# A cast and four copies moved to GpSimd, five steps moved within their lists, and a last product in two halves (attention and gated MLP, one core)

## The chip, the cores and the metric

The kernel runs on one core of one Trainium2 chip. A core has TensorE (PE in the profile; its weight loads are PEld), VectorE (DVE), ScalarE (ACT), GpSimd (POOL) and SyncE (SP), which here issues the transfers between the chip's memory and the core's SBUF. Every engine works through its own list of instructions in order and waits for the others by semaphores. The metric is the time of one execution in microseconds; lower is better.

## The reference

Eight batches, eight heads, 576 positions, head size 64. First attention in which a position sees itself and the 63 before it:

```
scores = matmul(q, k^T) / 8;  keep where 0 <= row - col < 64
attn   = exp(scores - max) / (sum + 1e-9)
x      = matmul(attn, v)          # heads side by side: [8, 576, 512]
```

Then a gated MLP with a product over positions:

```
h   = relu(x @ w_in)              # 1024 wide; u = first half, v = second half
v_n = (v - mean(v)) / sqrt(var(v) + 1e-6)
v_s = w_spatial @ v_n + b_spatial # over the 576 positions
out = (u * v_s) @ w_out           # [8, 576, 512], float32
```

All inputs and the output are float32; products are done in float16 with float32 sums.

## The kernel before

The code describes the work as named steps. The string ORDER is written out by hand: it lists every step once, with its engine and the numbers of the buffers it takes. The steps are issued in this order, so the list of each engine is the subsequence of ORDER with its name; DQ means a transfer on SP's queue. An engine's list is strict: an instruction that waits holds up all that are behind it. The names carry batch, head group (0 or 1, four heads each) and part.

For each batch and group:

- ldq, ldk, ldv load q, k (one transfer each, into one of eight buffers `nat`) and V (five transfers, positions in chunks of 128). The transfers of SP use eight semaphores in turn, so a transfer waits for the one issued eight places before it.
- cq, ck cast q and k to float16 (`cp`, line 301, or 293 on ACT; on POOL in three pieces of 384, line 296), tq, tk transpose them on DVE (line 408). cv casts V into `hv`; sl, su and s4 copy it into `hs`, shifted by half a chunk (lower half of the partitions, upper half, the last 64 positions). In batches 0 and 1 cv, sl and su come in two parts, 0 and 1 (su1_10 is batch 1, group 1, part 0).
- S (PE, line 470) makes the scores, E (ACT, line 477) their exp, M (DVE, line 480) applies the mask as a minimum, Z (PE, line 493) sums over columns, N and n (ACT, lines 519 and 521) give the inverse as exp of minus log, P (PE, line 504) multiplies with V from hv and hs, and X (DVE, line 512) scales into x. The steps with _r do the last 64 positions of both groups.

For each batch then:

- V (PE, line 643) makes the second half of h, Vr the relu (ACT, line 623), Vb and Va mean and variance (DVE, lines 625 and 627), L1 and L2 the inverse root (ACT), A the rescaling (DVE, line 682).
- U (PE, line 698) and Ur (ACT, line 711) make the first half, G (PE, line 728, the last columns 734) the product over positions, Ge (DVE, line 742) multiplies by u.
- O (PE, line 753) is the last product, Oe (ACT, line 606) copies it out of PSUM, st stores it. The last 64 positions of a batch share a step with V of the next batch (V_4: lines 656 and 659); those of batch 7 have none and are O7_4 (line 765): four products of 64 output rows and 512 columns, copied by Oe7_4 and stored by st7_4.

The three weights are loaded and cast between batches 0 and 1 (ldwin, cwin; ldwsp, cwsp, then W and We, which transpose the spatial weights; ldwo, cwo). ldb loads the spatial bias, cb casts it. NWARM = 25 pairs of products D on a scratch tile fill TensorE's waits in batch 0.

PSUM has two pairs of banks (for S) and four single banks, whose numbers 0 to 3 stand behind each PE step in ORDER. A step that takes a bank waits until the last reader of its former content is done: P1_11 takes bank 1, which Ge0_2 empties, and G0_2 takes bank 1, which X1_01 empties.

Of the kernel before, what the change touches and what calls it, by code (L numbers as in the profile page):

```python
# [13 lines left out]
B = 8  # L14
# [13 lines left out]
ldwin101:DQ D8:PE:1 su0_01:DVE sl0_01:POOL n0_10:ACT su0_10:DVE D13:PE:2 ldwin000:DQ:1 n0_01:ACT
tk1_0:DVE:5 s40_0:POOL ldk1_1:DQ:2 N0_11:ACT:4 P0_01:PE:3 ldq1_1:DQ:3 P0_00:PE:1 n0_11:ACT
cv0_11:DVE ldwin001:DQ S1_0:PE:0:1 sl0_11:DVE X0_00:DVE:0 D20:PE:2 cwin110:POOL ldwin010:DQ:4  # L30
E1_00:ACT:1 s40_1:DVE D19:PE:0 ldwin011:DQ su0_11:POOL X0_01:DVE ldwsp3:DQ:5 E1_01:ACT:0 M1_00:DVE
# [17 lines left out]
su1_11:DVE n1_r:ACT Ge0_2:DVE:2 P1_10:PE:2 n1_11:ACT X1_10:DVE:3 ck2_1:POOL:2 P1_11:PE:1 ldk3_0:DQ:2
S2_0:PE:1:0 X1_11:DVE cwo10:ACT ldv2_01:DQ P1_r:PE:2 Ge0_0:DVE:3 V1_2:PE:1 E2_00:ACT:0 X1_r:DVE:1  # L50
Ge0_1:DVE:4 E2_01:ACT:1 V1_1:PE:3 cq2_1:POOL:3 ldv2_02:DQ tk2_1:DVE:0 V1_3:PE:2 Vr1_2:ACT:5
ldv2_03:DQ cwo00:POOL Vr1_1:ACT:6 tq2_1:DVE:1 U1_2:PE:0 ldv2_10:DQ:1 Vr1_3:ACT:7 cwo11:ACT
ldv2_11:DQ V1_0:PE:1 M2_00:DVE Ur1_2:ACT:5 Vb1_2:DVE:5 cwo01:ACT S2_1:PE:1:0 Vr1_0:ACT:4 M2_01:DVE
Z2_00:PE:3 cq3_0:POOL:0 ldv2_04:DQ E2_10:ACT:3 V1_4:PE:2 Vb1_1:DVE:1 ldv2_12:DQ Va1_2:DVE
# [115 lines left out]
class Plan:  # L170
# [27 lines left out]
def kernel(  # L198
# [11 lines left out]
    nc = tc.nc  # L210
# [55 lines left out]
    w_out_sb = [cpool.tile([128, 512], f16, name=f"wout{r}") for r in range(4)]  # L266
# [331 lines left out]
    def out_steps(b, j, m, po, key, rows):  # L598
        half = j % 2
        if half == 0:  # L600
            OB[b] = (buf("ob", f"ob{b}_{j}") if j < 4 else buf("ob4", f"ob{b}_4")), None
        ob, first = OB[b]

        def view():
            return ob.t[rows, half, :] if j < 4 else ob.t[rows, :]
        cpy = add(f"Oe{b}_{j}", ("ACT", 0.49), key, lambda e: nc.scalar.copy(view(), m.t[rows, :]),  # L606
                  deps=[po, first], acq=[] if half else [ob], uses=[m] + ([ob] if half else []))
        OB[b] = ob, cpy
        if j == 4:
            add(f"st{b}_4", ("DQ", 0.45), key, lambda e: nc.sync.dma_start(  # L610
                out[b, 512:576, :], view()), deps=[cpy], uses=[ob], nbytes=0.4, n=64)
# [22 lines left out]
    def gmlp_steps(b, key):  # L634
        VS, ST, VN = [], [], []
        for j in range(4):
            m = buf("bank", f"pv{b}_{j}")
            vs = buf("vs", f"vs{b}_{j}")

            def emit_V(e, j=j, m=m):  # L640
                with nc.named_scope(f"V{b}_{j}"):
                    for r in range(4):
# [32 lines left out]
        for j in range(5):  # L675
# [4 lines left out]
            def emit_A(e, j=j, jn=jn, vn=vn):  # L680
# [8 lines left out]
        for i in range(5):  # L689
            m = buf("bank", f"pu{b}_{i}")  # L690
            ru = buf("ru", f"ru{b}_{i}")
            n = 512 if i < 4 else 256

            def emit_U(e, i=i, m=m):
                with nc.named_scope(f"U{b}_{i}"):
# [4 lines left out]
                    else:  # L700
                        for c in range(4):
                            for r in range(4):
# [10 lines left out]
        G = []
        gd = []
        for i in range(5):
            m = buf("bank", f"pg{b}_{i}")
            g = buf("g", f"g{b}_{i}")
            n = 512 if i < 4 else 256
            ru, rd = RU[i]

            def emit_G(e, i=i, m=m):
                def vk(kk):
                    return (VN[kk].t[:, :], 128) if kk < 4 else (vn4_t[b % NSB][:, :], 65)
                with nc.named_scope(f"G{b}_{i}"):
# [5 lines left out]
                    else:  # L730
                        for c in range(4):
                            for kk in range(5):
# [6 lines left out]
                     deps=AP + WSP, acq=[m], uses=[vn for vn in VN if vn], mode="f")  # L739
            gd.append(pg)  # L740
            G.append((g, add(f"Ge{b}_{i}", ("DVE", 0.07 + 0.00105 * n), key + 0.4 + 0.03 * i,
                             lambda e, m=m, g=g, ru=ru, n=n: nc.vector.tensor_tensor(  # L742
                                 g.t[:, 0:n], m.t[:, 0:n], ru.t[:, 0:n], ALU.mult),
                             deps=[pg, rd], acq=[g], uses=[m, ru])))
        GDONE[b] = gd
        G4[b] = G[4]
        for j in range(4):
            m = buf("bank", f"po{b}_{j}")

            def emit_O(e, j=j, m=m):  # L750
                with nc.named_scope(f"O{b}_{j}"):
                    for r in range(4):
                        nc.tensor.matmul(m.t[:, :], G[r][0].t[:, 128 * j:128 * j + 128],  # L753
                                         w_out_sb[r][:, :], start=(r == 0), stop=(r == 3))
            po = add(f"O{b}_{j}", ("PE", 0.866), key + 0.7 + 0.03 * j, emit_O,
                     deps=[G[r][1] for r in range(4)] + WOUT, acq=[m],
                     uses=[G[r][0] for r in range(4)], mode="f")
            out_steps(b, j, m, po, key + 0.7 + 0.03 * j, slice(0, 128))
        if b == B - 1:
            m = buf("bank", f"po{b}_4")  # L760

            def emit_O4(e, m=m):
                with nc.named_scope(f"O{b}_4"):
                    for r in range(4):
                        nc.tensor.matmul(m.t[0:64, :], G[4][0].t[:, 64 * r:64 * r + 64],
                                         w_out_sb[r][:, :], start=(r == 0), stop=(r == 3))
# [60 lines left out]
```

## Time and profile before

| what | value |
|---|---|
| median of 3 runs | 203.99 us (203.55 to 204.42) |
| the profiled execution | 204.42 us |
| its span, first to last instruction | 202.6 us |
| granted TensorE clock | 0.999 |
| PE busy | 189.1 us, 93% |
| ACT busy | 167.9 us, 83% |
| DVE busy | 162.4 us, 80% |
| POOL busy | 74.0 us, 37% |
| read from memory, written | 32.79 MB, 9.44 MB |

Busy times and shares are sums over the whole span; the slices and the windows of the trace tell in which stage an engine is full. The chain of waits follows the work that ended last back from the end of the span: at each step to what released it, or to the instruction before it on its engine. In the timeline, a row is a group of like instructions that follow each other: start, length, engine, line, operation, tiles, count, and in brackets the idle time of the engine before it with what ended that. Times on PE are modelled at the end of each product. A transfer's row on SPq is its issue; its landing is later.

### The profile page before, as it was taken

How to read it: one execution, taken by the hardware profiler on the slowest of the kernel's cores; microseconds unless marked ns; L12 is line 12 of the kernel's file. 1: busy time of each engine (PE TensorE's matmuls, PEld its weight loads, DVE VectorE, ACT ScalarE, POOL GpSimd, SP SyncE). 2: the span in 40 equal slices, each digit the busy share in tenths (PEclk: the TensorE clock that was granted, in tenths of full speed). 3: DMA queues.
4: the chain of work that ended last, by engine and by line, in shares of the span. 5: the costliest groups of instructions: out<-in, count | busy, mean ns of one | idle time of the engine just before them, and what ended most of it. 6: DMA issues, size and time to landing. Idle time of an engine off the chain costs nothing.

```text
span 202.6 us, 6997 instructions
## 1 busy us (share of the span) xinstructions
PE 189.1 (93%) x2923; PEld 97.7 (48%) x2923; DVE 162.4 (80%) x310; ACT 167.9 (83%) x308; POOL 74.0 (37%) x140
## 2 busy tenths in 40 slices
PE   7578899889999999999999999999999999999992
PEld 2233535545455544664554545554465555444450
DVE  4599979999999899799699898979957795647420
ACT  2578899894999899997998999999999999467342
POOL 5202565364795298335847998000000000000000
PEclk9999999999999999999999999999999999999999
DMA  6997999999896947998978993996623003200445
GB/s 226 359 264 195 309 386 223 289 375 380 174 268 230 297 147 202 262 295 207 343 178 208 271 331 129 229 299 229 184 107 116 3 5 131 107 0 0 161 131 179
DMA packets 50195, 42.69 MB, mean 211 GB/s; under 512 B 39345, under 2 KB 39345, under 8 KB 50162
## 3 DMA queue, kind: packets, MB, share of 16 engines
q1 hardware_dynamic: 50162, 42.23, 69.8%
q8 instruction: 23, 0.38, 0.8%
q14 instruction: 10, 0.08, 0.1%
HBM read 32.79 MB, written 9.44 MB: 208 GB/s over the span
## 4 chain that ended last, share of the span: by engine, by line
PE 73%; DVE 10%; DMA 8%; ACT 3%; issue 2%; SPq 1%; POOL 1%; POOLq 0%; ACTq 0%
PE bank L728 15%; PE bank L753 14%; PE bank L643 12%; PE bank L698 11%; DMA nq<-in_q_dram 4%; PE pair L470 4%; PE bank L504 4%; PE bank L493 3%; DMA nk<-in_k_dram 3%; PE bank L656 3%; PE bank L734 2%; PE bank L703 2%; DVE qT L408 2%; DVE st L625 1%; DVE hs L301 1%
## 5 line engine op out<-in xcount | busy, mean ns | idle before, releaser
L728 PE MATMUL bank<-wspT,vn 128*128 128x512 f16 (+1 forms) x160 | 37.7, 379 | 0.3 <-DVE x L512 0.3
L477 ACT ACTIVATE e<-pair 128x1024 f16<-128x1024 f32 x32 | 31.9, 1027 | 4.1 <-PE pair L470 3.8
L742 DVE TENSOR_TENSOR g<-bank,ru 128x512 f16<-128x512 f32 (+1 forms) x40 | 24.9, 632 | 11.0 <-PE bank L728 5.0
L698 PE MATMUL bank<-x,win 128*128 128x512 f16 x128 | 31.6, 379 | 0.0
L753 PE MATMUL bank<-wout,g 128*128 128x512 f16 x128 | 31.3, 379 | 0.0
L643 PE MATMUL bank<-win,x 128*128 128x512 f16 x128 | 30.5, 379 | 0.0
L711 ACT ACTIVATE ru<-bank 128x512 f32<-128x512 f32 (+1 forms) x40 | 21.4, 561 | 8.4 <-PE bank L698 4.6
L625 DVE BATCH_NORM_STATS2 st<-vs 128x6 f32<-128x512 f16 (+1 forms) x40 | 25.9, 670 | 2.9 <-ACT vs L623 2.6
L606 ACT COPY ob<-bank 128x512 f32<-128x512 f32 (+1 forms) x40 | 23.2, 588 | 3.7 <-PE bank L753 3.1
L623 ACT ACTIVATE vs<-bank 128x512 f16<-128x512 f32 (+1 forms) x40 | 23.0, 596 | 3.0 <-PE bank L643 2.1
L512 DVE TENSOR_TENSOR x<-bank,lz 128x512 f16<-128x512 f32 x32 | 21.3, 683 | 4.9 <-PE bank L504 2.3
L728 PEld LDWEIGHTS <-vn 128*128 128x128 f16 (+1 forms) x160 | 14.9, 97 | 18.3 <-issue 1.0
L480 DVE TENSOR_TENSOR e<-e,mask 128x1024 f16<-128x1024 f16 x32 | 22.8, 729 | 1.0 <-ACT e L477 1.0
L296 POOL CAST hq<-nq 128x384 f16<-128x384 f32 x33 | 17.2, 560 | 13.0 <-DMA nq<-in_q_dram 11.5
L408 DVE STREAM_TRANSPOSE qT<-hq 128x576 f32<-128x576 f32 x16 | 19.8, 1245 | 2.7 <-POOL hq L296 2.3
L408 DVE STREAM_TRANSPOSE kT<-hk 128x576 f32<-128x576 f32 x16 | 19.9, 1244 | 1.2 <-ACT hk L293 0.9
L519 ACT ACTIVATE lz<-bank 128x512 f32<-128x512 f32 x32 | 18.5, 600 | 1.8 <-PE bank L493 1.7
L521 ACT ACTIVATE lz<-lz 128x512 f32<-128x512 f32 x32 | 19.6, 630 | 0.1
L643 PEld LDWEIGHTS <-x 128*128 128x128 f16 x128 | 11.9, 98 | 14.2 <-issue 0.4
L698 PEld LDWEIGHTS <-win 128*128 128x128 f16 x128 | 11.8, 98 | 14.4 <-issue 1.3
L296 POOL CAST hk<-nk 128x384 f16<-128x384 f32 x27 | 13.9, 551 | 12.9 <-DMA nk<-in_k_dram 10.5
L682 DVE TENSOR_SCALAR vn<-vs,mv,ln 128x512 f16<-128x512 f16 (+1 forms) x40 | 15.4, 434 | 3.7 <-ACT ln L672 3.6
(84 smaller groups left out, 290.7 us busy)
## 6 DMA issues: line engine op xcount, KB each, us to landing
nq<-in_q_dram SPq DMA_DIRECT2D x16, 576.0 KB, 5.9
nk<-in_k_dram SPq DMA_DIRECT2D x16, 576.0 KB, 5.6
nv<-in_v_dram SPq DMA_DIRECT2D x64, 128.0 KB, 5.1
out_dram<-ob SPq DMA_DIRECT2D x14, 512.0 KB, 4.3
wi<-in_moe_w_in_dram SPq DMA_DIRECT2D x8, 256.0 KB, 4.7
ws<-in_moe_w_spatial_dram SPq DMA_DIRECT2D x4, 288.0 KB, 8.6
nv<-in_v_dram SPq DMA_DIRECT2D x16, 64.0 KB, 3.3
wo<-in_moe_w_out_dram SPq DMA_DIRECT2D x4, 256.0 KB, 6.8
```

The lines of the kernel that those rows point to most:

```text
L296: nc.gpsimd.tensor_copy(o[:, n:n + 384], i[:, n:n + 384])
L408: d = add(f"t{name}{b}_{g}", ("DVE", 1.09), key, lambda e: nc.vector.transpose(qt.t[:, :].rearrange("p (i j) -> p j i", j=18), h.t[:, :].b ...
L477: ex = add(f"E{b}_{g}{u}", ("ACT", 0.91), key, lambda e, u=u: nc.scalar.activation(e2[u].t[:, :, :], sc[u].t[:, :, :], AF.Exp, bias=0.0, s ...
L480: mins.append(add(f"M{b}_{g}{u}", ("DVE", 0.65), key, lambda e, u=u: nc.vector.tensor_tensor(e2[u].t[:, :, :], e2[u].t[:, :, :], mask[:, : ...
L606: cpy = add(f"Oe{b}_{j}", ("ACT", 0.49), key, lambda e: nc.scalar.copy(view(), m.t[rows, :]), deps=[po, first], acq=[] if half else [ob], ...
L623: rl = add(f"Vr{b}_{j}", ("ACT", 0.49), key, lambda e: nc.scalar.activation(vs.t[0:jn, :], m.t[0:jn, :], AF.Relu), deps=[pv], acq=[vs], us ...
L625: s1 = add(f"Vb{b}_{j}", ("DVE", 0.6), key + 0.02, lambda e: nc.vector.bn_stats(st6.t[0:jn, 0:6], vs.t[0:jn, :]), deps=[rl], acq=[st6], us ...
L643: nc.tensor.matmul(m.t[:, :], xr(b, r)[:, 128 * j:128 * j + 128], w_in_sb[r][:, 512:1024], start=(r == 0), stop=(r == 3))
L698: nc.tensor.matmul(m.t[:, :], w_in_sb[r][:, 128 * i:128 * i + 128], xr(b, r), start=(r == 0), stop=(r == 3))
L728: nc.tensor.matmul(m.t[:, :], w[0:kn, 128 * i:128 * i + 128], wspT[kk][0:kn, 0:512], start=(kk == 0), stop=(kk == 4))
L742: lambda e, m=m, g=g, ru=ru, n=n: nc.vector.tensor_tensor(g.t[:, 0:n], m.t[:, 0:n], ru.t[:, 0:n], ALU.mult),
L753: nc.tensor.matmul(m.t[:, :], G[r][0].t[:, 128 * j:128 * j + 128], w_out_sb[r][:, :], start=(r == 0), stop=(r == 3))
```

## The change

- ck1_0, the cast of k of batch 1, group 0, goes from DVE to POOL (there in three pieces), at the same place of ORDER.
- Four copies of V into hs go from DVE to POOL: sl1_01, su1_01, su1_10 and su1_11.
- Five steps stand elsewhere in their engine's list: ldb four transfers later on SP (behind ldwin000); su0_11 before cwin110 on POOL; M1_00 behind X0_10 and X0_11 on DVE; Z1_00 behind P0_r, V0_1 and V0_2 on PE; tk2_0 behind X1_01 on DVE.
- O7_4 makes the two halves of its 512 columns as separate products into the two halves of the partitions: eight products of 256 columns for four of 512, the halves in turn. Oe7_4 copies 128 partitions x 256 on DVE in place of 64 x 512 on ACT. Its store becomes two, of 64 rows x 256 columns, one from SP (st7_40) and one from ACT (st7_41). The store before it, st7_3, is issued from ACT.

The core of the diff (the lines of ORDER cut to the moved steps):

```diff
-... D4:PE:3 ck1_0:DVE:1 ldv0_13:DQ ...
+... D4:PE:3 ck1_0:POOL:1 ldv0_13:DQ ...
-... N0_01:ACT:1 ldb:DQ:0 M0_r:DVE ...
+... ldwin000:DQ:1 ldb:DQ:0 n0_01:ACT ...
-... cwin110:POOL ... su0_11:POOL X0_01:DVE ...
+... su0_11:POOL cwin110:POOL ... X0_01:DVE ...
-... E1_01:ACT:0 M1_00:DVE cwin111:POOL ... X0_10:DVE:1 ... X0_11:DVE cwin000:ACT Z1_00:PE:1 M1_01:DVE ...
+... X0_10:DVE:1 ... X0_11:DVE M1_00:DVE cwin000:ACT M1_01:DVE ... V0_1:PE:3 ... V0_2:PE:2 Z1_00:PE:1 ...
-s41_0:ACT su1_00:DVE We3:ACT sl1_01:DVE W1:PE:2 su1_01:DVE A0_2:DVE:2 ...
+s41_0:ACT su1_00:DVE We3:ACT sl1_01:POOL W1:PE:2 su1_01:POOL A0_2:DVE:2 ...
-... tk2_0:DVE:2 G0_3:PE:0 ... sl1_10:ACT:3 G0_0:PE:3 su1_10:DVE X1_01:DVE ...
+... G0_3:PE:0 n1_01:ACT X1_01:DVE tk2_0:DVE:2 ... sl1_10:ACT:3 G0_0:PE:3 su1_10:POOL ...
-su1_11:DVE n1_r:ACT ...
+su1_11:POOL n1_r:ACT ...
-Oe7_3:ACT st7_3:DQ Oe7_4:ACT:0 st7_4:DQ
+Oe7_3:ACT st7_3:ACT Oe7_4:DVE:0 st7_40:DQ st7_41:ACT
...
-        cpy = add(f"Oe{b}_{j}", ("ACT", 0.49), key, lambda e: nc.scalar.copy(view(), m.t[rows, :]),
+        last = (b, j) == (B - 1, 4)
+        cpy = add(f"Oe{b}_{j}", ("DVE", 0.4) if last else ("ACT", 0.49), key,
+                  lambda e: (nc.vector.tensor_copy if last else nc.scalar.copy)(view(), m.t[rows, 0:n]),
...
+        if j == 4 and b == B - 1:
+            for f, eng in enumerate(("DQ", "ACT")):
+                add(f"st{b}_4{f}", (eng, 0.45), key, lambda e, f=f: (nc.sync, nc.scalar)[f].dma_start(
+                    out[b, 512:576, 256 * f:256 * f + 256], ob.t[64 * f:64 * f + 64, 0:256]),
+                    deps=[cpy], uses=[ob], nbytes=0.2, n=64)
...
+            q = ("ACT", nc.scalar) if j == 3 else ("DQ", nc.sync)
...
                     for r in range(4):
-                        nc.tensor.matmul(m.t[0:64, :], G[4][0].t[:, 64 * r:64 * r + 64],
-                                         w_out_sb[r][:, :], start=(r == 0), stop=(r == 3))
+                        for f in (0, 1):
+                            nc.tensor.matmul(m.t[64 * f:64 * f + 64, 0:256],
+                                             G[4][0].t[:, 64 * r:64 * r + 64],
+                                             w_out_sb[r][:, 256 * f:256 * f + 256],
+                                             start=(r == 0), stop=(r == 3))
```

More of the change, by code (lines that the diff above doesn't have):

```diff
@@ L23 @@
 M0_01:DVE cq1_0:ACT:0 ldwin100:DQ:6 S0_1:PE:0:1 M0_00:DVE D5:PE:0 E0_10:ACT:2 tq1_0:DVE:4 D17:PE:1
-D2:PE:2 ldv0_04:DQ E0_11:ACT:3 D4:PE:3 ck1_0:DVE:1 ldv0_13:DQ D1:PE:0 S0_r:PE:0:1 M0_10:DVE
+D2:PE:2 ldv0_04:DQ E0_11:ACT:3 D4:PE:3 ck1_0:POOL:1 ldv0_13:DQ D1:PE:0 S0_r:PE:0:1 M0_10:DVE
 ldv0_14:DQ Z0_00:PE:1 E0_r0:ACT:0 cv0_10:DVE:0 Z0_10:PE:2 E0_r1:ACT M0_11:DVE ldwin110:DQ:7
-Z0_01:PE:3 N0_10:ACT:0 D10:PE:0 sl0_10:DVE:0 cv0_00:DVE:1 N0_01:ACT:1 ldb:DQ:0 M0_r:DVE N0_00:ACT:2
+Z0_01:PE:3 N0_10:ACT:0 D10:PE:0 sl0_10:DVE:0 cv0_00:DVE:1 N0_01:ACT:1 M0_r:DVE N0_00:ACT:2
 sl0_00:DVE:1 Z0_r:PE:2 su0_00:DVE ldwin111:DQ Z0_11:PE:0 N0_r:ACT:3 D9:PE:3 n0_00:ACT cv0_01:DVE
[L28 to L31, printed above, removed]
+ldwin101:DQ D8:PE:1 su0_01:DVE sl0_01:POOL n0_10:ACT su0_10:DVE D13:PE:2 ldwin000:DQ:1 ldb:DQ:0
+n0_01:ACT tk1_0:DVE:5 s40_0:POOL ldk1_1:DQ:2 N0_11:ACT:4 P0_01:PE:3 ldq1_1:DQ:3 P0_00:PE:1 n0_11:ACT
+cv0_11:DVE ldwin001:DQ S1_0:PE:0:1 sl0_11:DVE X0_00:DVE:0 D20:PE:2 su0_11:POOL cwin110:POOL
+ldwin010:DQ:4 E1_00:ACT:1 s40_1:DVE D19:PE:0 ldwin011:DQ X0_01:DVE ldwsp3:DQ:5 E1_01:ACT:0
 cwin111:POOL P0_10:PE:1 P0_11:PE:2 X0_10:DVE:1 D18:PE:0 cwin100:ACT cwin101:POOL ldwsp2:DQ:7 D3:PE:3
-n0_r:ACT X0_11:DVE cwin000:ACT Z1_00:PE:1 M1_01:DVE ldwsp1:DQ:6 P0_r:PE:0 cb:ACT V0_1:PE:3
-X0_r:DVE:0 V0_2:PE:2 ck1_1:POOL:2 ldwsp4:DQ:0 Vr0_1:ACT:0 N1_00:ACT:5 Vb0_1:DVE:0 V0_0:PE:0
+n0_r:ACT X0_11:DVE M1_00:DVE cwin000:ACT M1_01:DVE ldwsp1:DQ:6 P0_r:PE:0 cb:ACT V0_1:PE:3 X0_r:DVE:0
+V0_2:PE:2 Z1_00:PE:1 ck1_1:POOL:2 ldwsp4:DQ:0 Vr0_1:ACT:0 N1_00:ACT:5 Vb0_1:DVE:0 V0_0:PE:0
 Vr0_2:ACT:1 tk1_1:DVE:0 cq1_1:POOL:3 ldv1_00:DQ:2 V0_3:PE:3 Vr0_0:ACT:2 n1_00:ACT ldwsp0:DQ:2
@@ L43 @@
 Ur0_0:ACT:4 cv1_01:POOL W3:PE:1 We0:DVE ldv1_14:DQ sl1_00:ACT:2 We2:DVE ldk2_1:DQ:4 W4:PE:0
-s41_0:ACT su1_00:DVE We3:ACT sl1_01:DVE W1:PE:2 su1_01:DVE A0_2:DVE:2 We4:ACT Z1_r:PE:3 P1_01:PE:1
+s41_0:ACT su1_00:DVE We3:ACT sl1_01:POOL W1:PE:2 su1_01:POOL A0_2:DVE:2 We4:ACT Z1_r:PE:3 P1_01:PE:1
 A0_1:DVE:3 N1_r:ACT:0 We1:DVE ck2_0:POOL:0 ldwo10:DQ:5 P1_00:PE:0 Z1_10:PE:3 X1_00:DVE:2 G0_4:PE:2
-ldq2_1:DQ:7 N1_10:ACT:4 tk2_0:DVE:2 G0_3:PE:0 n1_01:ACT cv1_10:POOL:3 ldwo00:DQ:6 n1_10:ACT
-sl1_10:ACT:3 G0_0:PE:3 su1_10:DVE X1_01:DVE cq2_0:ACT:1 ldwo11:DQ Ge0_3:DVE:0 G0_2:PE:1 ldwo01:DQ
+ldq2_1:DQ:7 N1_10:ACT:4 G0_3:PE:0 n1_01:ACT X1_01:DVE tk2_0:DVE:2 cv1_10:POOL:3 ldwo00:DQ:6
+n1_10:ACT sl1_10:ACT:3 G0_0:PE:3 su1_10:POOL cq2_0:ACT:1 ldwo11:DQ Ge0_3:DVE:0 G0_2:PE:1 ldwo01:DQ
 Ge0_4:DVE:1 tq2_0:DVE:3 cv1_11:POOL ldq3_0:DQ:0 G0_1:PE:0 ldv2_00:DQ:0 s41_1:POOL sl1_11:ACT
[L49 to L54, printed above, removed]
+su1_11:POOL n1_r:ACT Ge0_2:DVE:2 P1_10:PE:2 n1_11:ACT X1_10:DVE:3 ck2_1:POOL:2 P1_11:PE:1
+ldk3_0:DQ:2 S2_0:PE:1:0 X1_11:DVE cwo10:ACT ldv2_01:DQ P1_r:PE:2 Ge0_0:DVE:3 V1_2:PE:1 E2_00:ACT:0
+X1_r:DVE:1 Ge0_1:DVE:4 E2_01:ACT:1 V1_1:PE:3 cq2_1:POOL:3 ldv2_02:DQ tk2_1:DVE:0 V1_3:PE:2
+Vr1_2:ACT:5 ldv2_03:DQ cwo00:POOL Vr1_1:ACT:6 tq2_1:DVE:1 U1_2:PE:0 ldv2_10:DQ:1 Vr1_3:ACT:7
+cwo11:ACT ldv2_11:DQ V1_0:PE:1 M2_00:DVE Ur1_2:ACT:5 Vb1_2:DVE:5 cwo01:ACT S2_1:PE:1:0 Vr1_0:ACT:4
+M2_01:DVE Z2_00:PE:3 cq3_0:POOL:0 ldv2_04:DQ E2_10:ACT:3 V1_4:PE:2 Vb1_1:DVE:1 ldv2_12:DQ Va1_2:DVE
 Vb1_3:DVE:3 U1_1:PE:0 Vr1_4:ACT:2 M2_10:DVE Oe0_4:ACT:0 O0_0:PE:1 ck3_0:POOL:1 ldv2_13:DQ
@@ L612, in out_steps @@
         elif b == B - 1:
-            add(f"st{b}_{j}", ("DQ", 0.45), key, lambda e: nc.sync.dma_start(
+            q = ("ACT", nc.scalar) if j == 3 else ("DQ", nc.sync)
+            add(f"st{b}_{j}", (q[0], 0.45), key, lambda e: q[1].dma_start(
                 out[b, 128 * j:128 * j + 128, :], view()), deps=[cpy], uses=[ob], nbytes=0.72, n=128)
```

7 lines of the change are left out of this document (4 added, 3 removed).

## The prediction

> **What bounds the kernel now.** Read in this order: the page's busy shares and slices, then busy time by stage, then the chain of waits, then single engines in the two stretches that the change touches.
>
> ```profile
> PE 189.1 (93%) x2923; PEld 97.7 (48%) x2923; DVE 162.4 (80%) x310; ACT 167.9 (83%) x308; POOL 74.0 (37%) x140
> ...
> DMA  6997999999896947998978993996623003200445
> ```
>
> The shares mislead as a mean: GpSimd (POOL) looks free and TensorE (PE) looks like the bound. By stage (us, then each engine's busy us):
>
> ```profile
> 36.00:47.40 11.40, 9.49 (x122) 5.42 (x122) 11.15 (x24) 8.28 (x17) 5.60 (x12) 1.00 1.02 349
> 47.40:80.00 32.60, 32.58 (x599) 17.03 (x599) 31.42 (x52) 30.09 (x56) 22.72 (x40) 1.00 0.82 233
> 80.00:120.00 40.00, 39.66 (x687) 21.24 (x686) 35.38 (x66) 36.91 (x71) 25.84 (x49) 1.00 0.95 259
> ```
>
> From 36.0 to 47.4 VectorE (DVE) is busy 11.15 of 11.40 us and PE only 9.49; from 47.4 on PE is busy without a break (32.58 of 32.60; the list of PE's waits from 48 on holds one of 0.3). So what comes off the path before 48 should move the whole rest forward, and only that. The chain says what the path is there:
>
> ```profile
> 19.84 6.58 DMA nk<-in_k_dram
> 26.54 1.41 POOL hk L296 x3
> 27.96 1.40 POOL hq L296 x3
> 29.39 1.26 DVE qT L408
> ...
> 38.47 0.29 DVE hs L301
> 38.79 0.28 DVE hs L301
> 39.11 0.29 DVE hs L301
> ...
> 41.55 1.17 DVE kT L408
> 42.75 0.73 DVE hs L301
> 43.51 0.69 DVE x L512
> ...
> 46.32 0.29 DVE hs L301
> 46.64 0.70 DVE g L742
> 47.38 0.44 PE bank L504 x16
> ```
>
> Two things are to be seen. Up to 29 the path is a transfer: k of batch 1 issued at 19.84, landed at 26.4, cast, transposed. After it DVE works its list with no idle time, and four of the five copies into hs in it (38.79, 39.11, 42.75, 46.32) are the ones that move; 38.47 (su1_00) stays.
>
> **Batches 0 and 1 up to 30 us: worth nothing, I take 0.** ck1_0 leaves DVE (0.74) for three POOL casts (3 x 0.51, less overlap 1.41). Its data lands at 14.2, POOL is idle from 6.26 to 19.00, and tk1_0 wants the result at 19.89, so it is hidden even at twice its time. The 0.74 goes to a wait: cv0_01 on DVE starts at 18.51 because its V landed at 18.52, whatever DVE did before. M1_00 behind X0_10 and X0_11 brings those 0.60 forward, but V0_1 (25.19) also needs cwin101, which ended at 24.98 after a landing at 24.31; at most 0.2 earlier. Z1_00 behind V0_2 delays N1_00 and the Vr0 relus queued behind it on ScalarE (ACT) by about 0.3; their readers on DVE come at 30.48 and later. All of this meets S1_1 at 30.70, which waits for tq1_1 and so for the transfer. su0_11 ahead of cwin110 still starts when cv0_11 ends (21.77); cwin110 and cwin111 slip to end near 23.8, before V0_1. ldb four places later on SP: three weight loads are issued 0.36 earlier, nk1_1 keeps its place and hour. Every SP transfer waits for the one eight places before, so ldwsp3 now waits for ldwin101 (24.3) instead of ldwin111 (issue at 23.20 before), 1.1 later, and ldwsp2 0.6 later; the transfers ahead of them still land at 26.4 to 30.4, so they queue in any case. cb then finds its bias in time (issued near 19.4, read at 25.6). Bounds: -0.7 (all of ck1_0) to +0.9 (below); I take 0, the landings being the rows at hand.
>
> **The four V copies, 38 to 48 us: -1.2.** Off DVE with their spacing: 0.32 + 0.32 + 0.76 + 0.32 = 1.72. On POOL each costs 0.63 to 0.73 (64x512 copies: 635 ns mean, 0.73 the longest at 19.00). POOL then runs:
> - sl1_01 38.25 to 38.9 (cv1_01 ends 38.19), su1_01 to 39.55, ck2_0 to 41.1 (before 40.96), cv1_10 to 41.7;
> - su1_10 waits for ACT's sl1_10 (42.15), to 42.85; cv1_11 to 43.5 (before 43.33); s41_1 to 43.95; su1_11 after sl1_11 (44.15), to 44.85; ck2_1 to 46.3 (before 45.77). cq2_1 waits for its landing at 46.82, so POOL's list has caught up there.
>
> They are not free for DVE, since it slows beside POOL:
>
> ```profile
> 42.72 0.62 POOL L301 CAST hv<-nv 128x512 f16<-128x512 f32 x1 [1.20 <-DMA nv<-in_v_dram]
> ```
>
> su1_10 ran from 42.75 to 43.48 against this cast and took 0.73 instead of 0.29; the two A0 rescales at 39.43 took 1.16 beside ck2_0 instead of 0.72 (as at 36.32). X, Ge and the transposes show no such stretch (tk1_1 beside hq's casts: 1.25). So su1_00 loses up to 0.44 to sl1_01 and A0_2 about 0.1 more than now: X1_00 starts near 40.55 instead of 40.88.
>
> X1_01 is next. It no longer stands behind tk2_0 and su1_10, but needs n1_01, thus N1_10, Z1_10, P1_00, P1_01 and su1_01, now 0.15 later (39.55 for 39.40). n1_01 ends at 41.5 (41.34 before): X1_01 41.5 to 42.2, DVE idle 0.3 ahead of it. Then tk2_0 (1.17, its input ready at 41.1) to 43.35, Ge0_3 0.6, Ge0_4 0.35, tq2_0 1.2, Ge0_2 0.65: 46.1 against 47.33. On PE G0_2 goes from 44.25 to 43.4, P1_10 finds su1_11 0.7 us early, P1_11 goes at 46.15 instead of 47.38, X1_11 ends at 47.4 and V1_2 starts then instead of 48.70. I take -1.2. Bounds: -1.7 (the whole 1.72, no stretch) and -0.3: POOL's longest stretched instruction (1.07 for a cast of 0.61, at 55.58) for each of the copies, which makes P1_01 0.9 late and X1_01 with it.
>
> Downstream, DVE and ACT move with PE. Transfers may not: the smallest room that I find is q of batch 4 (cast ends at 72.95, transposed at 74.9: 1.9) and V of batch 3 (last copy 82.75, P3_00 at 84.17: 1.4). Both exceed 1.2.
>
> **The last product, 197.5 us: -0.6.**
>
> ```profile
> 54.05 0.38 PE L656 MATMUL bank<-win,x 128*64 128x512 f16 x1
> 54.05 0.38 PE L659 MATMUL bank<-wout,g 128*64 128x512 f16 x1
> ...
> 197.55 1.05 PE L765 MATMUL bank<-wout,g 128*64 128x512 f16 x4
> ...
> 198.64 0.58 ACT L606 COPY ob<-bank 64x512 f32<-64x512 f32 x1 [0.40 <-PE bank L765]
> 199.25 0.47 SPq L610 DMA_DIRECT2D out_dram<-ob  x1
> ```
>
> The pair at 54.05 shows two 64-column products running side by side: 0.216 a pair, for 512 columns. Four pairs of 256 columns: 0.43 for 0.86, so PE ends 0.43 earlier (near 198.15). The copy of 128x256 on DVE, idle there: no such row; X_r and Ge of 128x256 take 0.42, the 64x512 copy on ACT 0.58: 0.16 less. DVE's pick-up after PE is 0.1 (Ge row at 194.28) where ACT's is 0.04. Copy done near 198.7 instead of 199.22: -0.53. The store's 0.47 of issuing is now two of 64 KB, one on SP, one on ACT behind st7_3, which ACT issues at 198.27 (0.34 as on SP; its list holds nothing behind st7_41 and only st7_3 before it), so both go at 198.7. Landing: 2.24 after issue for the old one, 2.05 to 2.07 for the 256 KB before it; I take 2.15, hence -0.6. Bounds: -0.9, and, as no ScalarE queue was ever used before, +2 (a load among busy queues takes 5.6 to 6.6 to land). From landing to span end 1.09 as before.
>
> **Sum.** 0 - 1.2 - 0.6 = -1.8 on the profiled execution: 204.42 to 202.6, span 202.6 to 200.8. It lay 0.43 above the median, 203.99; so 202.2.
>
> **Rivals.**
> - Only part arrives: a load or ACT's list holds PE up between 50 and 85 and gives the 1.2 back. For it: DMA busy 9 tenths in most slices to 120 us, rooms of 1.4 and 1.9. Against: SP's loads wait for stores and buffers that move too. 203.99 - 0.6 = 203.4.
> - DVE held for whole POOL instructions. For it: su1_10 ended 0.15 after the cast beside it. Against: the two A0 took 0.65 and 0.58 beside casts of 0.51 to 0.57, less than a wait and their own 0.40. If so, su1_00, A0_2 and A0_1 each wait one out, X1_00 ends 0.25 later than now (41.8), X1_01 near 42.4, and the term is -0.95: 202.5. The Trainium skill states this as a rule, page "SBUF — State Buffer", section "Who interferes with whom": VectorE in a two-port mode (copy, cast, tensor_scalar) and GpSimd exclude each other for the whole instruction, and the later one is fully blocked. By that rule the time would be 202.5; the stretched A0 rows agree with it in part only.
> - More: ck1_0's row is on the chain (0.74 at 14.97), so the start gains too: 201.5. Against: the landings at 18.52 and 26.42.
> - Slower: ScalarE's first transfers at the very end. If they take from issue what the loads' median of 5.6 to 6.6 shows, the tail is 3.5 to 4.4 longer: 203.99 - 1.2 - 0.5 + 3.5 = 205.8 or more. It turns the sign at 1.7 over the old landing. Against: nothing else is in flight there.
> - The shifted spatial-weight loads: if ldwsp3's 1.1 us passes on, cwsp0 (landed 35.74, on DVE at 35.95, room 0.2) holds DVE up by 0.9: 203.99 + 0.9 - 1.8 = 203.1.
>
> **How the numbers follow.** A measurement here tells about 0.5% (1.0 us) from no change. Forecast (201.6 to 202.9): 0.38; DVE held (202.5): 0.15. More (201.5): 0.08. Part (203.4): 0.21, spatial loads (203.1): 0.06. Slower (205.8): 0.12. Below 202.97 is faster: 0.38 + 0.15 + 0.08 + 0.03 (half of the spatial case) = 0.64; same 0.21 + 0.03 = 0.24; slower 0.12. The range from 201.4 to 203.7 leaves out the slower case and the edges.
>
> **What would show it.** Right: chain reaching PE near 46.1 instead of 47.4; V1_2 near 47.4; POOL copies of 0.6 to 0.75 at 38 to 45; the pairs of O7_4 0.11 apart, DVE's last copy near 0.4, last issues about 1.8 earlier. Wrong: V1_2 early but the last O7 product not; n1_01 or su1_11 late; a ScalarE store landing over 3 us after issue.

## The result, and the profile after

| what | before | after |
|---|---|---|
| median, measured beside each other (20 runs each) | 204.13 us | 202.14 us |
| after over before | | 0.9905, 95% interval 0.988 to 0.993 |
| the profiled execution | 204.42 us | 201.67 us |
| its span | 202.6 us | 200.0 us |
| its end of tq1_1 (transpose of q, batch 1, group 1) | 30.65 us | 30.31 us |
| its start of cwsp4 on DVE | 35.26 us | 34.31 us |
| from cwsp4 to the end of X1_11 | 13.37 us | 12.20 us |
| from V1_2 to O7_4 on PE | 148.85 us | 148.89 us |
| from O7_4 to the end of the span | 5.03 us | 4.51 us |

The kernel is faster by 1.0% (interval 0.7 to 1.2%). The medians are over all 20 runs; the ratio leaves out the slow ones, those over 1.5% above the fastest of their kernel (four of the changed kernel's). In the pair of profiled executions the difference is larger, 2.75 us, and the table says where it lies: 0.95 before cwsp4, 1.17 in the stage of the moved copies, 0.52 in the ending. The 148.9 us between carry the gain unchanged. The first 0.95 is not shown to be the change's. e1, e2 and e3 below, whose lists are those of the kernel before up to that point, start cwsp4 at 34.90, 34.52 and 33.95 (before: 35.26), and e4, which has the moved early steps, at 34.51. Of the 0.95, 0.34 is there when tq1_1 ends. The rest lies in two masks, M1_11 and M1_10; the timeline of DVE, before and then changed:

```profile
33.29 2.04 DVE L480 TENSOR_TENSOR e<-e,mask 128x1024 f16<-128x1024 f16 x2
...
32.96 1.43 DVE L480 TENSOR_TENSOR e<-e,mask 128x1024 f16<-128x1024 f16 x2
```

In the profile of before both masks ran beside GpSimd's casts of the spatial weights, whose start follows their landings. In e1, e2 and e3, with the same lists, the pair took 1.26, 2.05 and 1.25.

The busy shares, from the first lines of the page of the changed kernel, hardly tell anything:

```profile
PE 189.5 (95%) x2927; PEld 97.8 (49%) x2927; DVE 160.9 (80%) x306; ACT 166.7 (83%) x307; POOL 78.0 (39%) x147
```

VectorE (DVE) lost 1.5 us in all and GpSimd (POOL) gained 4.0: more work in sum, yet less time. The busy time by stage of the changed kernel (stretch, length, then busy us of PE, PE's weight loads, DVE, ACT and POOL, the granted clock, the DMA share and GB/s) shows where it counts:

```profile
34.31:46.51 12.20, 11.59 (x245) 7.14 (x246) 11.55 (x24) 9.73 (x23) 8.03 (x15) 1.00 1.03 333
46.51:80.00 33.49, 33.42 (x521) 16.93 (x521) 31.79 (x56) 31.84 (x60) 24.62 (x43) 1.00 0.86 242
```

In the stage of the copies TensorE (PE) is now as full as DVE (11.59 and 11.55 of 12.20), where over the same steps of the kernel before (35.26 to 48.62) it was busy 11.45 of 13.36 us and DVE 13.11. After it PE is full as it was, so nothing of the gain can be lost there except in a new wait. The chain of waits of the changed kernel says what sets the stage now:

```profile
37.06 0.44 DVE wspT L301
...
37.52 0.53 DVE hs L301
...
38.09 1.11 DVE vn L692 x2
...
39.22 0.45 DVE wspT L301
...
39.71 0.76 PE bank L744 x20
40.47 4.33 PE bank L738 x20
44.80 0.39 PE bank L504 x16
...
46.56 2.75 PE bank L653 x12
```

Of the five copies into hs that stood on the chain before, one is left (su1_00, 37.52). The chain is DVE's only as far as We1 (39.22). From there it runs through the products G on PE without a gap (39.71 to 44.80), then P1_10 and P1_11, the two X1 on DVE (not copied here) and V1_2 at 46.56. Before, PE waited three times in that stretch, for We1, for X1_01 and for Ge0_2, as the timeline of PE before shows:

```profile
41.01 0.76 PE L734 MATMUL bank<-wspT,vn 128*128 128x64 f16 x20 [0.83 <-DVE wspT L301]
...
44.25 2.33 PE L728 MATMUL bank<-wspT,vn 128*128 128x512 f16 x10 [0.32 <-DVE x L512]
...
47.38 0.25 PE L504 MATMUL bank<-e,hv 128*64 128x64 f16 x4 [0.44 <-DVE g L742]
```

The timeline of the changed kernel, POOL and then DVE, shows the copies where they went:

```profile
37.30 1.28 POOL L301 COPY hs<-hv 64x512 f16<-64x512 f16 x2
38.64 1.47 POOL L296 CAST hk<-nk 128x384 f16<-128x384 f32 x3
...
37.52 0.53 DVE L301 COPY hs<-hv 64x512 f16<-64x512 f16 x1
38.09 1.20 DVE L692 TENSOR_SCALAR vn<-vs,mv,ln 128x512 f16<-128x512 f16 x2
```

The pair on POOL is sl1_01 and su1_01, at 0.61 each. On DVE su1_00 beside the first took 0.53 (0.29 before), A0_2 beside the second 0.64, and A0_1 beside the first piece of ck2_0 0.64. Last the ending of the changed kernel:

```profile
195.45 0.63 PE L776 MATMUL bank<-wout,g 128*64 128x256 f16 x8
...
196.18 0.38 ACTq L623 DMA_DIRECT2D out_dram<-ob  x1
196.18 0.42 DVE L610 COPY ob<-bank 128x256 f32<-128x256 f32 x1 [3.58 <-ACT ob L610]
196.63 0.47 SPq L615 DMA_DIRECT2D out_dram<-ob  x1
196.64 0.55 ACTq L615 DMA_DIRECT2D out_dram<-ob  x1
```

The eight products of 256 columns take 0.63 us where four of 512 took 1.05, DVE's copy 0.42 where ACT's took 0.58. The last stores are issued 1.18 us after the start of O7_4 (before: 1.70). SyncE's landed 1.96 after its issue. ScalarE's landing is missing from this trace; in the six other runs with this ending that have it, it took 2.28 to 2.31. The bracket at DVE's copy names ACT's copy Oe7_3, which ended 0.03 earlier; the last product ended at 196.08, so the trace does not tell which of the two DVE waited for.

### The profile page after: what moved, and what is told of

The parts are those of the page before. It is cut to its first block, busy times and chain, and to the rows that moved or that the text cites. A ratio compares the mean times of both kernels' runs of the same rounds, so it can differ in the third digit from the quotient of the medians.

```text
span 200.0 us, 7013 instructions
## 1 busy us (share of the span) xinstructions
PE 189.5 (95%) x2927; PEld 97.8 (49%) x2927; DVE 160.9 (80%) x306; ACT 166.7 (83%) x307; POOL 78.0 (39%) x147
## 4 chain that ended last, share of the span: by engine, by line
PE 72%; ACT 9%; SPq 6%; DMA 5%; DVE 3%; issue 1%; POOL 1%
PE bank L738 18%; PE bank L763 13%; PE bank L653 12%; PE bank L708 10%; SPq L422 4%; PE pair L470 3%; PE bank L504 3%; PE bank L493 3%; PE bank L666 3%; DMA wi<-in_moe_w_in_dram 3%; PE bank L744 3%; DMA nk<-in_k_dram 2%; ACT vs L633 2%; ACT ru L721 2%; PE bank L713 2%; ACT e L477 1%
## 5 line engine op out<-in xcount | busy, mean ns | idle before, releaser
L610 ACT COPY ob<-bank 128x512 f32<-128x512 f32 (+1 forms) x39 | 22.6, 589 | 3.3 <-PE bank L763 3.1
L296 POOL CAST hk<-nk 128x384 f16<-128x384 f32 x30 | 14.8, 526 | 17.4 <-DMA nk<-in_k_dram 17.2
L763 PEld LDWEIGHTS <-g 128*128 128x128 f16 x128 | 11.8, 98 | 13.4 <-issue 0.5
```

The source lines that it names most:

```text
L296: nc.gpsimd.tensor_copy(o[:, n:n + 384], i[:, n:n + 384])
L610: lambda e: (nc.vector.tensor_copy if last else nc.scalar.copy)(view(), m.t[rows, 0:n]),
```

## The experiments

Theory: the copies give about 1.2 us in the stage of batch 1, the ending 0.5, everything else nothing, and the 149 us of PE's work between carry it. The rivals were that the gain lies in the early steps or in tk2_0, that it is given back on the way, and that DVE is held for whole POOL instructions. Each run below was timed beside the kernel before; "stage" is from the start of cwsp4 to the end of X1_11, and its column is split at the start of G0_4 on PE, the two parts adding up to it. All but the ratio are from the one profiled execution of each. In e13 G0_4 is counted from its second product, the first having run alone 0.57 earlier. e1 to e4 were timed together, so were e6 to e9 and e10 to e12; the kernel before beside them had medians of 204.34, 203.75 and 204.23 (203.71 beside e13), so small differences between ratios of different groups mean little. In e3, e6 and e9 cwsp4 itself was held, that is, it started but went on only when a cast of GpSimd was over, as e8 shows for another row (0.75, 0.91 and 0.91 us for 0.44), which is 0.3 to 0.5 of their "cwsp4 to G0_4".

| kernel | ratio to before, 95% interval | cwsp4 to G0_4 | G0_4 to X1_11 | ending |
|---|---|---|---|---|
| before | 1 | 5.75 | 7.62 | 5.03 |
| the change | 0.9905 (0.988 to 0.993) | 5.40 | 6.80 | 4.51 |
| e1, ending alone | 0.9998 (0.9963 to 1.0034) | 6.38 | 7.35 | 4.53 |
| e4, early steps alone | 1.0025 (0.9983 to 1.0068) | 6.15 | 7.19 | 5.03 |
| e2, copies alone | 0.9936 (0.9904 to 0.9968) | 5.51 | 6.79 | 5.03 |
| e3, copies and tk2_0 | 0.9939 (0.9907 to 0.997) | 6.06 | 6.80 | 5.03 |
| e10, without the ending | 0.9922 (0.9889 to 0.9956) | 5.16 | 6.79 | 5.04 |
| e6, stores on one queue | 0.9952 (0.9916 to 0.9988) | 5.87 | 6.80 | 5.08 |
| e7, k and q earlier | 0.9984 (0.9951 to 1.0018) | 5.40 | 6.80 | 4.58 |
| e8, one long cast | 0.9953 (0.9918 to 0.9988) | 6.04 | 6.80 | 4.50 |
| e9, su1_00 on POOL | 0.9942 (0.9908 to 0.9977) | 6.12 | 6.93 | 4.51 |
| e11, Z1_10 first | 0.989 (0.9847 to 0.9934) | 5.40 | 6.79 | 4.50 |
| e12, the change again | 0.9886 (0.9846 to 0.9926) | 5.40 | 6.80 | 4.51 |
| e13, We1 first | 0.9893 (0.9841 to 0.9946) | 5.55 | 6.79 | 4.52 |

**e1: the ending alone**

```diff
-Oe7_3:ACT st7_3:DQ Oe7_4:ACT:0 st7_4:DQ
+Oe7_3:ACT st7_3:ACT Oe7_4:DVE:0 st7_40:DQ st7_41:ACT
```

(with the code of the change for O7_4 and its stores)

> The kernel before with the new ending alone: O7_4 in two halves, its copy on VectorE, the two half stores, and the last two ScalarE stores. Theory (three terms add up: start 0, copies -1.2, ending -0.6): from the start of O7_4 to the end of the span 4.4 to 4.6 us where the kernel before has 5.03; in time -0.5 to -0.6, a ratio near 0.997. Nothing ahead of 195 us changes. Rival (a ScalarE store that lands late): its landing over 3 us after issue, that stretch 5.5 or more, ratio over 1. Second rival (the ending is most of the gain): ratio near 0.992.

The ending took 4.53 us in the profile, as expected. The times of this run show none of it (ratio 0.9998), though 0.5 us (0.9975) lies well within the interval.

**e2 and e3: the copies alone, and with tk2_0**

```diff
-... sl1_01:DVE ... su1_01:DVE ... su1_10:DVE ... su1_11:DVE
+... sl1_01:POOL ... su1_01:POOL ... su1_10:POOL ... su1_11:POOL
```

e3 besides moves tk2_0 behind X1_01 on DVE.

> The kernel before with the four copies on GpSimd alone, tk2_0 left ahead of X1_01. Stage: from the start of the cast of the fourth spatial-weight tile on VectorE (cwsp4) to the end of X1_11, 13.36 us in the kernel before and 12.20 in the changed one. Theory (VectorE's sum of work sets this stage): 12.0 to 12.3, for the order inside a list that never idles does not matter; ratio near 0.994. Rival (tk2_0's new place frees G0_2 and that is the gain): 12.9 to 13.3, ratio 0.998 to 1. Rival (VectorE held beside GpSimd for all that it saved): 13.0 or more.

> The four copies on GpSimd and tk2_0 behind X1_01, nothing else of the change. Stage from cwsp4 on VectorE to the end of X1_11: theory 12.2 as in the changed kernel, ratio 0.994; rival that the early steps of batches 0 and 1 are needed for it: 12.7 or more.

Both ratios are the same: the copies bring two thirds of the gain by themselves, and tk2_0's move brings nothing that shows. The stage of e3 was 12.85 instead of 12.2; the table says where: all of it lies before G0_4 (6.06). In that execution DVE came early to cwsp4 (33.95), waited 0.10 us for the landing of the next spatial weight, and had cwsp4 and su1_00 stretched beside POOL (0.75 for 0.44, 0.69 for 0.53). From G0_4 on e3 is as fast as the change. The 12.85 reaches the number of the rival (the early steps are needed: 12.7 or more), but e2, which lacks them too, has 12.30.

**e4: the early steps alone** (ck1_0, ldb, su0_11, M1_00, Z1_00)

```diff
-ck1_0:DVE:1
+ck1_0:POOL:1
...
-N0_01:ACT:1 ldb:DQ:0 M0_r:DVE
+N0_01:ACT:1 M0_r:DVE
...
-cwin110:POOL ldwin010:DQ:4 E1_00:ACT:1 s40_1:DVE D19:PE:0 ldwin011:DQ su0_11:POOL
+su0_11:POOL cwin110:POOL ldwin010:DQ:4 E1_00:ACT:1 s40_1:DVE D19:PE:0 ldwin011:DQ
```

(M1_00, Z1_00 and ldb's new place as in the diff of the change)

> The cast ck1_0 on GpSimd, and ldb, su0_11, M1_00 and Z1_00 at their new places; copies, tk2_0 and ending as before. Theory (the start is set by landings): 0, ratio 0.998 to 1.002; S1_1 starts within 0.1 us of the end of tq1_1, and tq1_1 follows the landing of q of batch 1 by 2.8 us as before; the stage from cwsp4 to X1_11 stays 13.4. Rival (ck1_0's 0.74 on the chain counts): ratio 0.9965. Rival (the later spatial-weight loads hold VectorE up): ratio 1.004, cwsp0 waiting on VectorE.

Nothing is gained, as forecast: tq1_1 ended at 30.57 (30.65 before). The three parts alone multiply to 0.996, give or take 0.006, against 0.9905 for all; the intervals meet, so these runs do not say whether the parts help each other.

**e10 and e12: the change without its ending, beside the change**

```diff
-Oe7_3:ACT st7_3:ACT Oe7_4:DVE:0 st7_40:DQ st7_41:ACT
+Oe7_3:ACT st7_3:DQ Oe7_4:ACT:0 st7_4:DQ
```

(with the code of before for O7_4 and its stores; e12 is the changed kernel, timed in the same group)

> The changed kernel with the ending of before: four products of 512 columns, copied by ScalarE, one store from SyncE. By my terms it lies 0.52 us (the difference in the profile, 5.03 against 4.51 from the first O7_4 product to the end) above the changed kernel measured beside it: ratio 0.993 where that has 0.9905. Rival, that the shorter ending does not reach the time: both the same.

> The changed kernel once more, beside the two others, as their measure: ratio 0.988 to 0.993, stage 12.2 us, ending 4.5 us. The time up to the end of tq1_1, which follows the landings, may differ by up to 1 us, as between the executions so far.

0.9922 against 0.9886, that is 0.7 us in the direction expected, with intervals that overlap. With e1 beside it, the time supports an ending worth something between 0 and 0.7 us; the 0.5 itself is a reading of profiles, where every one of eight endings with two queues took 4.50 to 4.58 us and every other 5.03 to 5.08.

**e6: the three last stores on one queue**

```diff
-Oe7_3:ACT st7_3:ACT Oe7_4:DVE:0 st7_40:DQ st7_41:ACT
+Oe7_3:ACT st7_3:DQ Oe7_4:DVE:0 st7_40:DQ st7_41:DQ
```

> The changed kernel, but its last three stores are all issued by SyncE, one behind the other; the halves of the last product and the copy on VectorE stay. My step: most of the 0.5 us came from the product and the copy, the second queue bringing little, since the last store is issued one place (0.4 to 0.5) later on SyncE but lands some 2.0 us after issue there instead of 2.3. So from the first O7_4 product to the end of the span 4.5 to 4.8 us (4.51 with two queues, 5.03 before the change), and the time within 0.3 us of the changed kernel, ratio 0.990 to 0.993. Rival, that it was the second queue that shortened the ending: 5.0 or more.

My step fell and the rival held: 5.08 us. The product and the copy were as short as in the change, and with three stores on the one queue it was of no use, as the ending of e6 shows:

```profile
197.66 0.42 DVE L610 COPY ob<-bank 128x256 f32<-128x256 f32 x1 [3.58 <-ACT ob L610]
198.41 1.11 SPq L615 DMA_DIRECT2D out_dram<-ob  x2
```

The copy was done at 198.08, but SyncE, which had begun to issue the store before (st7_3) at 197.65, began the next only at 198.41, and the last one 0.53 after it. Without st7_3 in the way it would have begun at 198.11, as ACT and SP do in the change. Why SyncE took 0.76 us from one issue to the next, where ACT began its next 0.46 after st7_3, no view shows. e6 issues one store more from SyncE than the kernel before; the short product with a single last store was not run, so what product and copy are worth without the third issue stays open. Its time, 0.9952, is also above the 0.990 to 0.993 expected.

**e7: k and q of batch 1, group 1 asked for one transfer earlier**

```diff
-ldwin000:DQ:1 ldb:DQ:0 n0_01:ACT tk1_0:DVE:5 s40_0:POOL ldk1_1:DQ:2 N0_11:ACT:4 P0_01:PE:3 ldq1_1:DQ:3
+ldb:DQ:0 n0_01:ACT tk1_0:DVE:5 s40_0:POOL ldk1_1:DQ:2 N0_11:ACT:4 P0_01:PE:3 ldq1_1:DQ:3 ldwin000:DQ:1
```

(and cwin000 directly before cwin001)

> The changed kernel with ldwin000 four transfers later (behind ldq1_1) and its cast cwin000 later in ScalarE's list, so that k and q of batch 1, group 1 are asked for one transfer earlier. My step says that up to 30 us the path is the landing of these two: then they land 0.5 to 0.7 us earlier, the transposes (tq1_1) end near 29.7 instead of 30.3, the list of VectorE behind them begins that much earlier, and the whole is 0.3 to 0.6 us faster than the changed kernel: ratio 0.987 to 0.989. Rival: the list behind is held by the landings of the spatial weights (near 30.8 to 32.5) and their casts on GpSimd, then tq1_1 is early and nothing else: 0.9905.

tq1_1 ended 1.04 us earlier than in the change (29.27), and cwsp4 started only 0.22 earlier. The chain of waits of e7 names what took the place:

```profile
30.24 0.49 ACT vs L633
...
30.76 0.69 DVE st L635
...
32.52 0.92 DVE e L480 x2
33.44 0.66 issue
34.09 0.42 DVE wnat L301
```

DVE waited 0.42 us for a relu of ACT's list. The 0.66 called issue is no idle time of DVE: in it the mask M1_10 ran on, from 33.05 to 34.17, so 1.12 us for the 0.66 of the mask ahead of it, beside GpSimd's cast of a spatial weight that ended at 33.63. So the landing of k and q is one of several bounds that lie within a few tenths of each other, and the casts of the spatial weights on GpSimd are among them, as the rival said. The time fits neither expectation: 0.9984, with an interval wholly above the change's, although the profile is the shortest of all (span 199.3). Why the runs are slower than that one execution stays open.

**e8: POOL casts k of batch 2 in one piece**

```diff
-lambda e: cp(e, h.t[:, :], n.t[:, :])
+lambda e: (nc.gpsimd.tensor_copy if (name, b, g) == ("k", 2, 0)
+           else lambda o, i: cp(e, o, i))(h.t[:, :], n.t[:, :])
```

> The changed kernel, but GpSimd casts k of batch 2 (ck2_0) as one instruction of 1152 elements instead of three of 384; all in all it takes about as long (1.4 us against 1.47). The rescale A0_1 on VectorE starts within it. If VectorE only slows down beside GpSimd, A0_1 stays at 0.64 us and everything else with it: stage from cwsp4 to X1_11 12.2 us, ratio 0.9905. If VectorE is held until GpSimd's instruction is over, A0_1 ends some 0.14 us behind the long cast, takes 1.5 to 1.6 us, X1_00 ends 0.9 later, X1_01 loses its 0.3 of idle time and starts 0.55 later: stage near 12.75, time 0.4 to 0.6 us longer, ratio 0.993.

This tells the two readings of the stretched rows apart. The timeline of e8, DVE, then POOL, then PE:

```profile
37.62 1.84 DVE L692 TENSOR_SCALAR vn<-vs,mv,ln 128x512 f16<-128x512 f16 x2
...
38.17 1.14 POOL L406 CAST hk<-nk 128x1152 f16<-128x1152 f32 x1
...
39.88 0.76 PE L744 MATMUL bank<-wspT,vn 128*128 128x64 f16 x20 [0.99 <-DVE wspT L301]
```

The second rescale (A0_1) took 1.28 us of those 1.84 instead of 0.64 and ended at 39.46, 0.15 after the cast (which took 1.14, not the 1.4 that I had put down). So DVE does not slow down in proportion beside POOL; A0_1 was held until POOL's instruction was over. G0_4 starts 0.64 later, and the stage is 0.64 longer, 12.84. This is the rule of the Trainium skill, page "SBUF — State Buffer", section "Who interferes with whom" (a copy, cast or tensor_scalar of VectorE in a two-port mode and an instruction of GpSimd exclude each other, and the later one waits the other out): the trace agrees, with A0_1 ending 0.15 after the cast.

**e9: the fifth copy, su1_00, on POOL too**

```diff
-su1_00:DVE
+su1_00:POOL
```

> The changed kernel with the fifth copy into hs of that stretch, su1_00, on GpSimd too, ahead of sl1_01. If VectorE's list still sets the stage, it loses the 0.53 that su1_00 took: stage from cwsp4 to X1_11 near 11.7 us, ratio 0.988. If the path has moved to GpSimd's copies (su1_01 would end 0.65 later, so would P1_01 on TensorE, and through Z1_10 and the inverse n1_01 the start of X1_01, near 41.1 instead of 40.55): stage near 12.7, time 0.3 to 0.6 us longer than the changed kernel, ratio 0.992 to 0.993. I expect the second.

The second expectation held. DVE reached We1 early and then had nothing to do; the two X1 on DVE in e9:

```profile
39.63 0.69 DVE L512 TENSOR_TENSOR x<-bank,lz 128x512 f16<-128x512 f32 x1 [0.83 <-PE bank L504]
40.93 0.69 DVE L512 TENSOR_TENSOR x<-bank,lz 128x512 f16<-128x512 f32 x1 [0.61 <-ACT lz L521]
```

PE had to wait for su1_01, now third in POOL's list, before P1_01, and G0_4 stands behind that on PE: 6.12 instead of 5.40, and a stage of 13.05. Of this, 0.47 is not the fifth copy's but the hold of cwsp4 in this execution. Counted from the end of cwsp4, DVE ended We1 0.58 earlier than in the change, G0_4 still started 0.24 later, and the stage was 0.38 longer. A fifth copy is one too many for POOL's list.

**e11 and e13: two attempts at a faster version**

```diff
-P1_00:PE:0 Z1_10:PE:3
+Z1_10:PE:3 P1_00:PE:0
```

> The changed kernel with the sums Z1_10 ahead of P1_00 on TensorE. X1_01 waits 0.29 us for the inverse n1_01, which comes from su1_01 on GpSimd through P1_01, P1_00, Z1_10 and N1_10. If that is what sets the stage now, n1_01 ends 0.2 earlier and the stage from cwsp4 to X1_11 is 12.0 us, the idle time ahead of X1_01 0.1; in time 0.2 us, too little to tell. If VectorE sets it otherwise, 12.2 as it was.

The idle time ahead of X1_01 fell from 0.29 to 0.09 us, and the stage stayed at 12.19. X1_01 is no longer on the path; G0_4 still started 5.40 after cwsp4.

```diff
-su1_00:DVE ... A0_2:DVE:2 ... A0_1:DVE:3 ... We1:DVE
+su1_00:DVE ... We1:DVE A0_2:DVE:2 ... A0_1:DVE:3
```

> The changed kernel with We1, a copy out of a PSUM bank, ahead of A0_2 and A0_1 in VectorE's list. The runs so far say that TensorE's products G0_4 start when A0_2, A0_1 and We1 are done (5.40 us after the start of cwsp4), run without a break to P1_10 and so set X1_10 and X1_11; that the A0 are held by GpSimd's copies; and that a copy out of PSUM beside GpSimd is not (0.44 us). Then We1 runs while A0_2 would have stood held, all three are done near 5.0 instead of 5.35, G0_4 starts right behind Z1_10, 5.05 behind cwsp4, and the stage from cwsp4 to X1_11 is 11.9 us instead of 12.2; in time 0.3 us, ratio 0.987 to 0.991. Rival, that the list of VectorE from X1_01 on (which waits for n1_01 as before) sets the stage: G0_4 early, stage 12.2.

A miss. The idea was to let the copy out of PSUM, which POOL does not hold, run in the time in which A0_2 would have stood. It did run unheld (0.46), and A0_2 then started behind su1_01. But POOL has no gap there: in e13 both rescales met the three pieces of ck2_0 instead,

```profile
38.64 1.12 DVE L692 TENSOR_SCALAR vn<-vs,mv,ln 128x512 f16<-128x512 f16 x2
...
39.82 0.74 PE L744 MATMUL bank<-wspT,vn 128*128 128x64 f16 x19 [0.37 <-DVE vn L692]
```

0.62 and 0.59 each, one piece each, and G0_4 went on at 5.55. Neither version beats the change: e11 had 0.989 beside its 0.9886, and e13, measured apart from both, 0.9893.

What a gap would be worth, e10 shows without having been made for it. There k of batch 2 landed at 38.83, so its cast on POOL began at 38.98, 0.11 after A0_1 on DVE. The timeline of e10, DVE and POOL:

```profile
38.31 0.96 DVE L682 TENSOR_SCALAR vn<-vs,mv,ln 128x512 f16<-128x512 f16 x2
...
38.98 1.55 POOL L296 CAST hk<-nk 128x384 f16<-128x384 f32 x3 [0.18 <-DMA nk<-in_k_dram]
```

A0_1 took 0.40 of the 0.96, and it was the cast that was held (1.55 for 1.40). G0_4 started at 5.16, and the stage was 11.95, the shortest of all. A cast of k that waits for A0_1 on purpose was not tried.

## Why the prediction was right

Forecast 202.2 us, -1.8; measured 202.14, and by the ratio -1.94 against the kernel before beside it (interval -2.45 to -1.43). By its steps:

- **Start, 0:** right in the sum (e4, 1.0025 with an interval that holds 1). ck1_0's 0.74 on the chain, the rival "more", brought nothing.
- **Four copies, -1.2:** -1.17 in the profiled stage, 1.3 us (0.65 to 2.0) in e2's time. The working in between holds as well when counted from cwsp4, since everything ahead of it came 0.95 earlier: X1_00 at 5.29 forecast and 5.27 found, n1_01 ending at 6.24 and 6.20, the idle time ahead of X1_01 0.3 and 0.29, the end of X1_11 at 12.14 and 12.20. V1_2 stood at 46.56 instead of the 47.4 forecast only because of those 0.95.
- **But not by the path that the step named.** It let DVE's list carry the stage through X1_01, tk2_0 and Ge0_2 to P1_11. In the traces that list sets the time as far as We1 (G0_4 starts at 5.40); from there PE's products G set the rest, 6.8 us in every kernel with the four copies on POOL (6.93 in e9 alone), and 7.2 to 7.6 without. e11 shows that X1_01 has slack. The path that the step named was hardly shorter: Ge0_2 on DVE ended 0.09 before P1_11 started on PE. Two paths of nearly the same length gave the right number, and that was luck.
- **"DVE held for whole POOL instructions", put as a rival at 0.15:** its mechanism is what happens (e8), and my ground against it was misread. I took "less than a wait and their own 0.40" as evidence against a hold; but a held rescale ends 0.14 to 0.15 after POOL's instruction, not 0.40. Its price was over-sized for the same reason: it asked for X1_00 0.25 later than before, and X1_00 came 0.35 earlier, counted from cwsp4 (the A0 pair paid the hold already before the change: 0.65 and 0.59; only su1_00's 0.24 is new). So the forecast's sum stood with the rival's mechanism.
- **Last product, -0.6:** -0.52 in the profile. The issue came 0.52 earlier, as worked out (0.53); the landing was mis-sized: 2.15 was taken, SyncE's store took 1.96 from issue and ScalarE's 2.28 to 2.31 in the runs that show it, so the later of the two gave back what the smaller store should have brought. In the times the term is not shown: e1 and e10 leave it anywhere from 0 to 0.7. The bound of +2 for an unused queue did not come near.
- **Downstream, 0:** PE carried 148.85 and 148.89. "Only part arrives" did not happen in the change. Over all profiles the same stretch took 149.15 us on average with the copies moved (11 profiles, 148.4 to 150.0) and 149.05 without (3). Three of the eleven hold a wait of PE of 1.0 to 1.2 us, e3 near 115 us (the last point of this document), e6 and e9 near 125 for X on DVE. For the last two the traces show what came before. A mask on DVE with both operands in SBUF, 0.41 alone, got its turn only when several GpSimd instructions in a row were over; the timeline of e6, DVE and POOL:

```profile
116.63 3.52 DVE L553 TENSOR_TENSOR er<-er,maskr 128x512 f16<-128x512 f16 x1
...
116.69 2.28 POOL L299 CAST hv<-nv 128x512 f16<-128x512 f32 x4
118.92 1.59 POOL L296 CAST hk<-nk 128x384 f16<-128x384 f32 x3
```

The same mask took 0.55 to 1.77 us in the three profiles without the moved copies and 0.89 to 3.88 in the eleven with them (2.51 in the change). PE waited near 125 only where it took 2.96 or more: 0.26 in e13, 1.08 in e6, 1.18 in e9. So a way to lose part of the gain does exist, by DVE and not by a load or ACT as the rival had it; how often the runs take it, and whether the moved copies make it longer, is not shown.

- **Spatial-weight loads:** cwsp0 was not late (in e1, with the old order, DVE waited 0.35 for it); ldwsp3, issued 0.8 later on SP, landed earlier than before (30.75 for 31.85).

What the prediction did not see is how much a single execution owes to landings and to which instructions meet: it forecast 202.6 for the profile, which showed 201.67, and nearly all of that difference is the 0.95 before cwsp4.

## What to carry to other kernels

Before moving a copy to GpSimd, list which instructions of VectorE from SBUF to SBUF will run beside it: in these traces each was held until the GpSimd instruction that it met was over, and one mask until seven were (e6). So short GpSimd instructions, in stretches where VectorE reads PSUM, are the cheap ones. Count a moved copy as gained only as far as the next path allows: here 1.72 us left VectorE and 1.17 arrived, because su1_00's hold took 0.24 and TensorE's run of products then set the end. At the end of a kernel, when the last store is cut in two, give the halves queues that are free when the data are ready: on one queue the shorter product and copy brought nothing in the profile (5.08 for 5.03).

## What the runs showed of the hardware

- A rescale or copy of VectorE of 512 float16 elements from SBUF to SBUF that started in this stage while GpSimd ran ended 0.14 to 0.15 us after GpSimd's instruction, however long that was (1.28 us beside a cast of 1.14, 0.64 beside a copy of 0.61). Others ended later behind it: the cast cwsp4 0.31 (e3, e6, e9), the mask M1 of 1024 elements 0.54 (before, e7). If VectorE was first, GpSimd waits (e10).
- The mask er (512 elements, both operands in SBUF) was passed over by GpSimd instructions that follow each other closely: in e6 seven (a copy, four casts of V and two of the three pieces of k) ended before it got through, 0.28 behind the last of them. The rescales A0 met such a row of casts too and were held by one piece each (e13). What makes the difference was not tested.
- Copies out of PSUM beside GpSimd kept their 0.44 to 0.46 us. The Trainium skill, page "VectorE: DVE Perf Modes", section "Why PSUM operands drop a tier", says that an operand in PSUM shuts out the mode that needs both ports; the unheld copies agree with it.
- One cast of 1152 elements on GpSimd took 1.14 us, the same in three pieces 1.40 to 1.47. Beside VectorE the pieces are still the better choice: the stage was 0.64 shorter with them.
- Two sets of 256-column products into the two halves of the partitions took 0.63 us for the 1.05 of four of 512.
- ScalarE's last store of 64 KB landed 2.28 to 2.31 us after its issue (six profiles), SyncE's of the same size, issued within 0.01 us of it, 1.94 to 2.01 (eight). ScalarE had issued a store of 256 KB 0.46 before; whether the engine or that store makes the difference was not tested.
- In the middle of one run of score products near 115 us PE stood still for 0.1 to 1.0 us in eight of the fourteen profiles, released by nothing that the profile shows. In all eight a transfer on the queue that the page calls q8 instruction ended 1.3 to 1.7 us before the wait was over; that it is the cause was not tested.
